# New costs for the SyncE transfers in a planned Trainium2 kernel, and another order of all its tasks

## The chip, the cores and the metric

The kernel runs on one core of a Trainium2 chip. The core has a matrix engine (TensorE, PE in the profile; its weight loads are PEld), VectorE (DVE), ScalarE (ACT), GpSimd (POOL) and SyncE (SP), which issues transfers. Each engine takes its own instructions in order; they wait for each other through semaphores. The metric is the time of one execution on the device in microseconds (us), as the median of three runs. A profiled execution gives a span, which is the time from the first to the last instruction of the program.

## The reference

Two layers are applied twice, A (attention with a recurrent memory) and B (a gated feed-forward), each to the layer-normed activations and with a residual. The weights are the same both times.

```python
def _A_ref(x, mem0, Wq, Wk, Wv, Wo, seg_len):     # x: 1 x 2048 x 512
    mem = mem0                                    # 8 rows
    for s in range(n_seg):                        # 64 segments of 32 rows
        h = concat([mem, x[segment s]])           # 40 rows
        q, k, v = h @ Wq, h @ Wk, h @ Wv          # 32 heads of 128
        p = softmax(mask(q @ k.T * scale))        # memory rows are seen by all, the rest is causal
        o = (p @ v) @ Wo
        mem = o[:8]; outs.append(o[8:])           # the next segment needs this memory
def _B_ref(x, w_gate, w_up, w_down):              # 512 -> 1792 -> 512
    return (sigmoid(x @ w_gate) * (x @ w_up)) @ w_down
x = x + _A_ref(_layernorm(x), ...); x = x + _B_ref(_layernorm(x), ...)
x = x + _A_ref(_layernorm(x), ...); x = x + _B_ref(_layernorm(x), ...)
```

A segment of A can't begin before the segment ahead of it has given its eight memory rows. This makes a chain of 64 segments in each of the two passes.

## The kernel before

**Steps.** The two passes run interleaved: in step t (`emit_step`, 70 steps) the first pass works on segment t and the second on segment t-6 (`LAG`). From step 6 to step 63 both are present and a step has 80 columns, 40 of each. Before and after that it has 40. After every fourth step of a pass comes the feed-forward of the 128 rows that are then complete (`ffn`), whose gate, up and down weights are streamed from HBM in pieces by GpSimd (L1140, L1141, L1165).

**One step.** The 32 heads go in six groups. For each group TensorE makes Q and K (L923), ScalarE copies them to the tile `qku` (L944, carried out at L1285), TensorE makes the scores (L958), VectorE and ScalarE the softmax (L972 to L989), TensorE transposes it (L1001), two copies spread it into `ptsb` (L1279 or L1287 on VectorE, L1277 or L1285 on ScalarE), TensorE multiplies it with V (L1028), ScalarE copies the result into `otsb`, and TensorE multiplies it with the output weights (L1046). The last copy of a step (L1059, VectorE) writes the new memory rows into the input `hT` of the next step.

**V.** The V rows that do not depend on the memory are made ahead, for whole blocks of 128 rows (`v_pass`, `v_half`, `v_strip`), and stored in a scratch tensor in HBM, `scr` (L727, L764, L774; those of L727 and L764 are issued at L1281). In its step each such set of rows is loaded from `scr` into the tile `vsb` (L892, "rows" below, 24 rows of 1024 elements). The V rows that depend on the memory are made in the step by the matmuls of `strips` (L837), copied to `sst` and moved to their partitions of `vsb` by transfers (L903, "strips"). L1028 needs both. There are three `vsb` tiles, and a step uses two, so that a row transfer waits until L1028 of an earlier step has read its buffer.

**Saved columns.** In steps 0 to 5 the Q and K of 14 columns of the second pass are made along and saved (`kx`, written to the tensor `xq` at L952). In steps 6 to 11 they are loaded again (L871) and copied into `qku`. The blocks of x are loaded at L814.

**Order.** Nothing is emitted in the order in which `trace` names it. Each call `pl.add(engine, duration, function, r=, w=, lat=, nb=, slow=)` makes a task, with the tiles that it reads and writes, its issue time, for a transfer its latency until the data has landed (`lat`), its bytes (`nb`), and a share `slow` of the time for which weights are still streaming that is added to the latency. `Planner.plan` decodes the string `SEQUENCE` into a priority for each task. `forward` then plays all tasks through: whenever an engine is free, it takes the ready task with the highest priority, and a task is ready when what it needs has ended by the planned durations and latencies. So the emitted order on each engine follows from both, the priorities and the costs. The choice between ScalarE and VectorE for a copy, and between SyncE and GpSimd for some stores at the start, falls in the same way. SyncE is planned with at most eight transfers on their way.

**Fillers.** Where the plan leaves TensorE idle for over 250 ns at the start or after a thin stretch, `warm` puts matmuls of a constant tile in (L1271). They do nothing but keep the array busy.

The lines of the costs before:

```python
{"SP": 450, "POOL": 590} if boot else (400 if n == XS else 650)    # L727, store of V rows to scr
lat=1750.0 if b < 2 else None                                      # L814, x block; None is 4000
lat=3000.0                                                         # L873, kx
pl.add("SP", 375, ...), lat=2425.0, nb=nx * 2048, slow=1.0         # L892, rows
pl.add("SP", 600, ...), lat=2800.0, nb=nr * 2048, slow=0.6         # L903, strips
```

Of the kernel before, what the change touches and what calls it, by code (L numbers as in the profile page):

```python
# [20 lines left out]
P = 128  # L21
MEM = 8
SEG = 32
L = MEM + SEG
LW = 2 * L
XS = 24
# [28 lines left out]
;AsOfI9&h>01L}@xdvLQE|92eUGM9vk>p6h1lsKkB^29CMlL#^u9wB%1;X1aT-yCr)h^vqn{ccqtPEvUe^t*qOXz+z_UfSyR<kN<%R+NE9&QHjj<pdSp3CgCAC3h8^)yHKKrAEbzD2^vK#Fyn>oiLZcveBE4i53u  # L55
SI7gpgiO8+0q_g7z1dxxZw32ChqmxZj3++bjM=LtK&{Rp{IoUSeU|-iQe-$^np+3y*U~5|vmroI2|{3Q%S6U<M8?h}*J#6~ePFa&ILsP!iu)7M5zN}^;Hu*SkiWLt*l(;S-RciTt7j;!OclX8)R5sKu~O_HD!r1+
jCIF}*+yMG1QFSz)a{%7Adp3>lEB~B=MtoL428l7*eg@LBRPg-nsQ6v)y9;i>$(UC(aBy(o!AIwl~I$cgq8W9Wp}GPr0+oN?n!J3?D*{wW@2=s#eTk~wKe8QE?=WSX#u&mTeg#vYy?Rp>C(hv&bz%?pbf?=b}MF_
eO$W+#>2rveRa&s{$Nm5nNlpBy-Iu*4?_dWf<v!4+(q#pEwMk%5Z|67@u_WH)YDU;(8!QhOARUI@Ev$x`u@x*jByPk@sLpOC&1#RVOJh$lj(bC1d{d*)swiuXTt}spz40;rOBLuJ`uD7xa-ZjG9Qx~Yhb)>0}@{&
oqYugl(zT%&|W5_&rYr^Hs5H<BVhK1#NR7T%m9eQo~P9*BixidoIm{z#)5bD<m=G2*^@zhpvf?l?}6Jkr-@v|hw1`SI+F<rNj>J`)+W5o*fp+rSu#D|P&7rp7aWAwxHxlgc;$!At7$s0u0dZ^>Q%|9b*OUG)Kd|V
a#F;OGGzIJe_kq^-IMRF%TQ8m0V;(+iN9N8`!Z(hCvYtwB_4$P8RayXB@L8NkY6qJJ9Vova$FJfB0xcz@`1-gjGZ4TwAWQm9lDkE4=en>PiYLyavFTU=8P;Ni7bkPUF~y{NT^sK?@nuP27qn2(Tbj=pUwpTd&wfr  # L60
;vn+p55I)krt8@^*b8H{Na;xc%~``DuWGkVk<Cm}R-CrQWZ`4;;dgT-{$Z*q<}1{&a1+T=@Slz8iZkI!S}eXyae}BoI*xmDI$28yNQRH9k!T9ZU8In??!x!83EW{8W>+1ejosWwfq3Lztd9o%7-t8kDJi>B>kDo4
eA-oCu|dTIF0BkK8reW}fQfx1j)VzS{gg`C!j&(&+O4wh3;F|@Yg{6^dgkYz%bglXMBOw2Aix2(ih;~{9G(66p~AZp=^Nq#Y<a-pr#!Nxtbx3PEZ7H%#WJDmq&nPd-PGt|Ywo<+&t{#{Nt7b0Bro&6of$r~>_v*_
9ras2J?7d?<RRtFusz7ln=>9h5h*N8NdQP6gP0BT$`55r91aYXaXIs2J1S9u?PTNkIa-q3w6YsU45c`#(ULHdpV*82^@euSg-ey#+=oxlHqN7Sf1StR14}+-7k8vg31_)kSvwhIt{pJ=_g5=kZQ~5BiM8FSEM?TX
pew0R6uF&$gf2qG;Cc)$gt=i7B24}e^N7Qq&$QN9wh~FBXT(58?j$v!`}J+dR4M!OsI0aUFo&@+%@9*A1JMR{zI-ZkUTG_yKFpSCWC|QpET?5wHOAjV30aJg%K)6k1;l(IHMtS0l^gj!<sKedb<zs8Ls?wEXh6fR
xIk(E4Pn<UMX;SrNj!<=L3?t84g=8fclD#7yj1VnuQ)7HbC`_QE)1?eLH#3Zs3Qz9P-FL^xU7?_nXg_&$@O|uYAp9j|9NE5<U^nSVLoL=j>3j*lkzI%LR*H|&8kw_$5gp?6JL~o9)n@O3E#B~6h{smtD*LmlPLl+
G)A(n^s3wmvf_OiM#;Ngxr1tczZY9^2K5F~+diMwKC<0q_9-D-?iBWAN2@Jb7?MIXZ~`4_A-p_6!#<yO+!|<JJR+7irZ5M&yA<Iz1FdFEKGcduJ{LT}-2}46EMz%$^iB^sUP)`!E}d~eNTAfS;*erAk5GI~-fu0Q
?tH?Yg9_>H51&URf=fln2iLSM#P<G!+*l~+VXq1GfL;wEH-t>+$CK>q|7AAW!K5&nTclK_^z_V|Pt5?6sx7=#!p?+HGHaVhxd7;2Y$g6b?NBextlu{vpKQccKk!JtuXVKECWP|BDTc853cOD3QGVnb9JqZ1tdu%V
(F#;aw#){W_e{TALuP$|+*!(5dgLq81pH~AIj~fxqm^SFug_03%!Io0zYcU6%6B-5wRf!*EbmtDIL~~cGF|bSH=VwIq}W1F#F1KM9jgBp2yZBeIu?Jow<5O@oeu!)<<XGbXy^Ob;9C8D-gJ&zYCuxwmb5y_Yuf|D
7}wYFM?_6qWGcocqWEiarEaf%+&a9>Nk@OiNST3--;KAuM-5qY{1Q+<8)iR5Jt6C-L9oao+>myjNFjM7j8j9PA~cs5f@q+c`~5|qVl(NbM|YPcXdG)V-5L?3%+132)cvOuQ;?s*9n*Y$5^E=pKHsnhWP94xv3$1l
{XWA(vcG(Wg$1AFZX6f5U#qQpeM|B<8bL${mhLb{$Ixi#f?S5+AV_YMnGfxG)<ff!h((g449-Smtw=wOZWkkg>uW)2WNMhfFJSHVC?tCk(?;@LzKGlgIE1?URop&83VKNohpzu{3JOTpCEFV`?4(@PY7Y-WB5YO0  # L70
ge1R4!Cyl^sxzc>&O1xr9_FkR4C~_hE)m<kIDeNr+P+l?<|(tG^eJSe@>nSVP1KStG3Wu7t&p0~?GSXWKO>@O65VygJ{3P<pZbSC=Sq)aT?c1M&8#?h{Zrs!9OPF~Te}`);5oSv-?cM~my)puyS*6Gz;xD>&JgL6
f99KHg26|z9O9LYxhpg4(Ba}7LeK=2jggLK);OgbD)Q3g(mCF!Ht)VJ8XTImVtKXw^`@-vnN>GjmB_NeEvZjb++L-$j}5u+ozFGq>I>^W!Auz5`B7)W9%cKS#G&tH;tEb=RaKBlF@N1j&mUYoKr)t@4+O36`eZtX
iDt+VkT-z}d%<+E5>F1vkR~DDGfJ)N`x(@+z9)3Wb*LtmnRKVF%TnAfE%cf0Rs!7}iA`{XIyYH_-38im5MI=KA2>-7@vH4RPL1gyE2mkiDQ|nGb2VI|8)hSq9+QTZ6`_Zc1EQ5a*}0hf7zFN<(+~HIYO_M`1yDLg
;jR2VHx=(yXnloyVX|?t3?OHu$&Dg(-DZKM)brogA-E$daDdz93la4qafiHI8xPrgB{kAz-z^Tu+Y=!8lOov50Py+FLNkih=5_oPD<*_{&-Ra!G3<ss69&hs!WK2ZtkowL`0=K=w|gHqfBoC0Q28sf`szN$y}`gx
kc2YE1b^><;3lZh#sw@SU>9%;g84-{)@CWwy4L1n%Z?@!*e%WaA60tbAwO&g?ub}MWxk3aNIU4_xv=)i*Rt894VY!mHgb?=u%xLt!_z^fTyDX9%e2>G^a$E`Tj1~C^lx&X+MA9fSK#GmAVdK51M$*Ia6~{jsS7NP
qIM`znQ>9Pxk=T7yRDB$1`zD06*ZYT()R%<H6p1C9O1?Hxo+7jaR{W4SU*?NFLMZ1>$-dCt}<Y{!NNv5R;vQneRZw*OS#~6$cP2SLVl@F?9#Ot&Uu6eyqlqgYPz{;R+|ySzeT8bOx~7x*n4ptRNJ{2!S`|@%A<WV
&K^P&(BSiUsT&T(wamON<vNZXjp=g6zy%}u2SBja4|y6sv23s_)@G=(sQY!g6ItpKa@+V+Iy$+7ZCUQtU5u6oD3ovRcI~g}gb`__5EIOs(A|uDXe&nw-Z0Sg4*{0~XQY2?Z)s_wS?uLSCSiQyNf|D2<M8>M_Phy~
l&(%&GK;0>m-W!f;$z8l>eM?cMyU`$r4M_7qE<p8*j7)FY=dIdd^`_xy|c`l9;UsRpPctVXoN~qK^G5j0wjC>V1CI4_lM$Y$+Gh5T)A~SQsFpYTJ1TKfwS`&c^oSrd|iv`Y^t%_2MY88dQFY6{=uDZ$It)nX&Q*b
5~$(|eq~y`Z}Eg(p)oZ%DJrL$?b~gPaKUM1n&odK{$O*|u$}UE>~-ybtz|KVon*3!S`t;F8=^$4rf0e*m!kb)Rt|3#X4e{gx7_S$;mpaiB_F9;rX=NH$AfP{E#(F+0|MC*_w8!=2f4pQ6uq{GqR8cRpKieqE>lc9
yg(7S3B>|v5rq};V4)w>R*$xRb8tz?#SsW1gS0IfGsn9Jy#@t<ufLaus^Q;2JfZqYO4x7jjJ>I;0~wb(zMC6d^NeNgAa3&G<=|T4Ec!gc6|FvO*$@zJ+f!r=0_ULM6r$$e%$7nBjIHu-sZro(7$1~aqH`wS)-OuW  # L80
{+mk!BvS}f^3loSi5ZruZusL~;=l?m$B%7j&2N)X0bacAg@%`RmM^!|f9J7nm1i7b(&z@J^#22Jdl?22yNV^WQ4D@wWl)!k2bLUFMYhr=CF9wbc%1@hX<e0%<q02J)b%WBy)KMIbz%VHzqPVD*~WL+_-dPc3k#~M
WqjsYp{><~v`tgNn~#Z0`Q;jflJelAc3~vr1wbsFlAdiY@3>UDBY^(9Eg3cGhx51IJ~&7o^e0=*cl&a!_*^l&E|uQOk)bM~_G_Mnr4ag$Paf~f5+z$f3az65APw>TuvKV|C^F(MSnY`UD1}92R_j<4DN|a4-DhX!
zJEHNIg3bioKJV54ndGl|9=to>{~@dv06wfY4#EO9!G1Q04LKqY8<0c)`EBdsZ-bN$=UXc4115<p!k<{+fonl8uGELTtt+BBnv|`$U*Vzn-r=7goM_3c4OXk;bVJ1@!}4G4XKkpLsr+ygTK*??$3|i?KFdg1XQ0D
Z_~HfW(&zo4?e{S>CgE(@tpqYK%Y~5MjgVEf!U0Y0XwSS&dGoKdK<hnVUDGM>1yhkpfD2AQ&lT*?r+ahN*TV6q_6~HZ<^{q3;E>=st<F@zb!DQ1ck!;MF_aR?OoIz9R?+%JJ{(S`CR|9Lh0HJoy8XHL9b=J^sngt
BAM@2iepOh4q6Ny_5hNTBEBrCDHto}0TOFSVeCNPCRs+UYrsQfp5VsAbY1!&_iVoB664azU}iZ{{%cTTyK(Y|fh1i`LOigZRtXYOiq_}GHDAnmV0|4vp2UDU4ym*2d`oKtNRKmUnt|Tzcc%32UNrR_qWEr*s}y<@
_w5%QvSS$$Pk9G=gwHK$EZ^8IrDS3)T*bz$amn&zIEYUcftc4d6(gP89~GN-&J8F@Pfk^VFHOx>S~%_f;>!I<c88F}^m3Z_pFRk#33GY>$1zjyXQQOlIeyz>CMBM-?5&UBAK;+%jZD-FCFu;!y|)A|jLeHE5%?|z
D+KX&`1g2$BX19j0BM;#yL_OVErdZTl3_}GmPuw`goJy5D=2k+zY||~^NkAEEf;&*!~2_+(V>M&M3QRJ1MiMD;bY&4^;7?|81U-xuZ<#B^6Ak6x-B3_1uhvg$@dp}SArA7AwaiC1*Xp~N*fiAiNhyhq~2S5?5BWR
Hn)s(s^P`!%;StBs0Z=dg3|4TN$Sno_d28Rl)%_3)Lv}oJXK)JPH!l7UqXOWraL;}T1bBSN|N<Tm=yH{GGwyK2SB6IG!P23f5oKJ81RJhJ{&B_>QeFTy2mpqi!T{ZZ70M!!jTIZtx8;Hy>zndA%4$uzRBj|5mh-4
GVG#Mnf-F8;t$fa;h*2>HOsW3m1#dzyc5!8C^j!VkC`D(0eHwFW%P$goCXjNi_-8Y0%)wy@VJ|jatlVBtarW{zNy`L&_~sQ{**^F2i~+wVZ5>L_GCZSJi59y7W;c}3()6{DjG5?HI0T0u}j3$lQWXjkywU5LuV=W
;pIjJe)F+93SjcWX{PO1*8iP(y{pkU>wSy}vz=|Y70|uh;!pS%Ft86nIYI1Z9urWikohb4fpC_w^P>i;@i;DsOCYP^;7<q(KEn-8S%8$}vH(ND4ZV$o(mdW90<r7)L_lOh?CT<ly;-B&9#?ic-I+8$F?(Hyahvgt  # L90
<fsyZpo^y~;MhAKv(-Mo1LStkt0^fT$w7QiMBMmEXpxAq$GNj<KZ#;rKwzNGJ^1AayX!tq-0)Dx*}VTALVxT1trNk8adW5O9SERf25ro`u`h(X4ULpde<B3_4d2Z&0%Ku1OBO;kIT77sq>8$C-wG8ao6XYS%48R}
_|gTLU>_PS>8L~Mil=Q50*O^Di#S>GL9p|}!LtZbc%WJ3b#;)yJIx}w@B@+$^PdMky1+6#ll|l|fv=R8(L|T2U!fJw1iXP@kv|ZC?8Tp;#4P&<ej=7_l#xmW=cz_Nk;A36MlutxZ%n3#8hBidXUboGhbrV0d!LqP
9xzAQ(-Zd&y}_5`hG^`Gw>ryv|17uDhspjsr|D*4V<d$}nK;;O`jFTA^-^KHH$kA1^tIOScC1{YQ)g@K8A&7MVXZ*ht#<5KrBc3>SmC}(M<OqE{q!i$3y*-*{s)fBwhWt({gE&KIQT9`n*yn&ns{CVq+WCIN962k
y&0PGK}(xZx2q4r!R+TLZS3XJa;6mEI<-7V$=`16g+qefBI1VAfa?q4uke&936N?96AvC(HCW#kD%V&4lvL%t(+mw?Z2bcDpFr)wy2PzYBrtO087>97Zkkx&@8rOq*~%Ouj?);**JT%QNmR@dY#yIb!<be5)>;2)
b9!_~e`QYSYszG<yb;W^!Ki|4>6;e0OrQ|w9cd=_=!BCSXRrMsYbG@15T+~!n+;rr0sg>NOadJGSnPJR+;~{I4>xS$cyug3A`I)QL)*&d<<;O3FN(atVB3X`wBzWR3`$l$qc+{9!4{8&c`koXmrTXeXDhzvy&JiJ
y#rp5#pe7u<Hg|ibJcUKMfEKdlZB3{(X*qk?wC5BShIbp-k8R5{_!z{+~FE)KT?57Er8DQKea|Fig_=qnmt$K4ZC!2<r8lrV3*(KFBT@PJ(6+3Jp^DVF^PyfoE#<eb&)=0=HR{&bw#U-Gl7GJ=?u`!md-jhLhOTs
A}u)t+OP)^&OmaUwTXH&5{cqXZL&`gdvGdI=ZF_-qr7?n;lxdZj9Fw7FVZIZDi9r8plwgl3>Bhm<Rta*y%y*+@PL=lqa&t91ps<#H28%kG5c9s!xRMuQ-b(esOr4NhcpTM0|3F4?HtST9Nd+&f(XRe2qiJcZV1e<
# [367 lines left out]
class Kern:  # L465
# [237 lines left out]
    def v_pass(self, tile, keys, pieces, boot=False):  # L703

        nc, pl, DC = self.nc, self.pl, self.DC
# [645 lines left out]
```

## Time and profile before

| | |
|---|---|
| median of three runs | 1791.44 us (1787.53 to 1792.42) |
| the profiled execution | 1786.9 us |
| its span | 1785.1 us |
| TensorE busy | 1762.3 us, 40081 matmuls |
| VectorE, ScalarE, GpSimd busy | 1171.3, 1170.9, 575.6 us |
| strips, `vsb<-sst` (L903) | 516 transfers: 464 of 32 KB, 48 of 64 KB, 4 of 48 KB |
| rows, `vsb<-scr` (L892) | 508 transfers: 460 of 48 KB, 48 of 16 KB |
| granted TensorE clock | 0.999 |

Matmuls overlap in the records: each is shown with its full latency of about 0.2 us, while the next one starts when the array can take it. Busy time is the union of the records. A wait is put down to the semaphore that came last. "issue" stands for idle time in which the engine waited for nothing that the profile shows. SPq is SyncE's queue: the time of an entry is that of the issue, not of the transfer.

### The profile page before, as it was taken

To read this page: it belongs to the slowest core of one execution; us is meant where nothing else is said; L and a number is where in the kernel's file an instruction comes from. 1 tells how busy PE (TensorE), PEld (TensorE's weight loads), DVE (VectorE), ACT (ScalarE), POOL (GpSimd) and SP (SyncE) were. 2 spreads that over 40 slices of the span, in tenths; PEclk is the share of its full clock that TensorE was granted. 3 is DMA by queue.
4 is the path that set the end of the run, shared out by engine and by line. 5 is a ranking of instruction groups with operands and counts; after the bars stand their busy time and mean duration, and the time that the engine had idled before them with its cause. 6 is when DMAs were issued, how large, how long until landed. Compare 5 with 4: busy or idle time off the path is not lost.

```text
span 1785.1 us, 92363 instructions
## 1 busy us (share of the span) xinstructions
PE 1762.3 (99%) x40081; PEld 1510.4 (85%) x40081; DVE 1171.3 (66%) x4002; ACT 1170.9 (66%) x3040; POOL 575.6 (32%) x831
## 2 busy tenths in 40 slices
PE   9999999999999999999999999999999999999998
PEld 4578788989888898889888898989888888889886
DVE  4376666677576666666666677657766766666675
ACT  6676766666666666766666666666666666666664
POOL 5313032422333242323324241333325132333432
PEclk9999999999999999999999999999999999999999
DMA  9835354644555464545546453555546454554543
GB/s 347 276 89 153 84 163 136 192 115 131 160 157 156 131 183 130 142 131 161 163 126 196 131 169 101 157 157 168 153 132 195 113 147 126 156 158 131 170 131 107
DMA packets 135305, 273.43 MB, mean 153 GB/s; under 512 B 30778, under 2 KB 68546, under 8 KB 134898
## 3 DMA queue, kind: packets, MB, share of 16 engines
q0 software_dynamic: 56384, 182.30, 34.8%
q1 hardware_dynamic: 78514, 85.22, 16.6%
q8 instruction: 314, 5.14, 1.2%
q14 instruction: 93, 0.76, 0.1%
HBM read 221.78 MB, written 27.07 MB: 139 GB/s over the span
## 4 chain that ended last, share of the span: by engine, by line
PE 91%; DMA 3%; DVE 2%; SPq 2%; ACT 1%; issue 1%; POOL 0%; ACTq 0%; POOLq 0%
PE bank L923 30%; PE bank L1046 17%; PE bank L1148 11%; PE bank L713 8%; PE bank L837 7%; PE bank L1171 5%; PE bank L1028 4%; PE bank L958 4%; PE bank L1001 2%; DMA vsb<-sst 2%; SPq L903 2%; PE bank L1271 1%; PE bank L673 1%; PE bank L1116 0%; DMA kx<-xq 0%
## 5 line engine op out<-in xcount | busy, mean ns | idle before, releaser
L923 PE MATMUL bank<-hT,wq_sb 128*128 128x80 bf16 (+3 forms) x8960 | 614.9, 198 | 1.0 <-DVE hT L1059 0.6
L923 PE MATMUL bank<-hT,wk_sb 128*128 128x80 bf16 (+3 forms) x8960 | 614.8, 198 | 0.8 <-issue 0.8
L1285 ACT CAST qku<-bank 128x480 bf16<-128x480 f32 (+4 forms) x770 | 387.5, 507 | 220.2 <-PE bank L923 183.0
L923 PEld LDWEIGHTS <-wq_sb 128*128 128x128 bf16 x8960 | 452.4, 99 | 26.5 <-issue 13.7
L923 PEld LDWEIGHTS <-wk_sb 128*128 128x128 bf16 x8960 | 446.9, 99 | 1.2 <-issue 1.2
L972 DVE TENSOR_TENSOR st<-bank,cst 40x240 f32<-40x240 f32 (+2 forms) x768 | 277.4, 367 | 169.7 <-PE bank L958 162.8
L1046 PE MATMUL bank<-otsb,wo_sb 128*128 128x80 bf16 (+1 forms) x8960 | 363.5, 198 | 3.3 <-ACT otsb L1285 1.8
L1046 PEld LDWEIGHTS <-wo_sb 128*128 128x128 bf16 x8960 | 336.8, 99 | 18.5 <-issue 3.8
L1140 POOL DMA_DIRECT2D wg<-in_B_w_gate_dram x217 | 163.9, 755 | 281.5 <-PE bank L1148 79.1
L1141 POOL DMA_DIRECT2D wu<-in_B_w_up_dram x217 | 164.2, 757 | 262.6 <-PE bank L1001 70.2
L1285 ACT CAST otsb<-bank 128x480 bf16<-128x480 f32 (+3 forms) x420 | 198.7, 483 | 72.2 <-PE bank L1028 48.2
L1165 POOL DMA_DIRECT2D wd<-in_B_w_down_dram x217 | 153.8, 709 | 199.2 <-PE bank L1171 48.5
L982 ACT ACTIVATE st<-st 80x240 f32<-80x240 f32 (+3 forms) x420 | 158.6, 381 | 30.6 <-DVE st L979 28.8
L984 DVE TENSOR_REDUCE small<-st 80x6 f32<-80x240 f32 (+3 forms) x420 | 151.2, 363 | 35.7 <-ACT st L982 33.9
L1148 PE MATMUL bank<-xnT,wg 128*128 128x128 bf16 (+2 forms) x1784 | 171.6, 218 | 0.3 <-DVE xnT L1287 0.3
L663 POOL TENSOR_TENSOR small<-small,cst 128x1 f32<-128x1 f32 (+1 forms) x80 | 45.1, 565 | 392.1 <-DVE small L662 389.2
L1148 PE MATMUL bank<-xnT,wu 128*128 128x128 bf16 (+2 forms) x1784 | 171.3, 218 | 0.2 <-issue 0.2
L958 PE MATMUL bank<-qku 128*128 128x80 bf16 (+1 forms) x2240 | 160.7, 198 | 0.8 <-ACT qku L1285 0.4
L979 DVE TENSOR_TENSOR st<-st,small 80x240 f32<-80x240 f32 (+3 forms) x420 | 153.9, 369 | 4.0
L989 DVE TENSOR_TENSOR pb<-st,small 80x240 bf16<-80x240 f32 (+3 forms) x420 | 153.1, 369 | 4.3
L977 DVE TENSOR_REDUCE small<-st 80x6 f32<-80x240 f32 (+3 forms) x420 | 151.1, 362 | 4.3
L1028 PE MATMUL bank<-ptsb,vsb 104*128 104x80 bf16 x2048 | 138.3, 199 | 6.5 <-DMA vsb<-sst 3.1
(105 smaller groups left out, 2409.9 us busy)
## 6 DMA issues: line engine op xcount, KB each, us to landing
wg<-in_B_w_gate_dram POOLq DMA_DIRECT2D x220, 256.0 KB, 4.3
wu<-in_B_w_up_dram POOLq DMA_DIRECT2D x220, 256.0 KB, 4.3
wd<-in_B_w_down_dram POOLq DMA_DIRECT2D x220, 256.0 KB, 4.2
vsb<-scr SPq DMA_DIRECT2D x460, 48.0 KB
vsb<-sst SPq DMA_DIRECT2D x464, 32.0 KB
scr<-vst SPq DMA_DIRECT2D x112, 96.0 KB
wv_sb<-in_A_Wv_dram SPq DMA_DIRECT2D x8, 512.0 KB
wo_sb<-in_A_Wo_dram SPq DMA_DIRECT2D x10, 384.0 KB
```

Source lines behind the costliest of these rows:

```text
L923: nc.tensor.matmul(o_ap, lhsT=W[:, c, h * P:(h + 1) * P], rhs=mv(c), start=(c == 0), stop=(c == DC - 1))
L958: nc.tensor.matmul(s_all(SB)[:, w0 + i, :], lhsT=fview(qku[:, i, 0, 0:1], [(1, P)]), rhs=qku[:, i, 1, 0:ncol], start=True, stop=True)
L972: pl.add("DVE", dve_ns(n, True), lambda gsz=gsz, hs=hs, st=st, SB=SB, pj_=pj_, npj_=npj_, mk=mk, idx=idx: nc.vector.tensor_tensor(out=st[p ...
L979: pl.add("DVE", dve_ns(n), lambda gsz=gsz, hs=hs, st=st, mx=mx: nc.vector.tensor_tensor(out=st[pr, hs], in0=st[pr, hs], in1=mx[pr, hs].uns ...
L982: pl.add("ACT", act_ns(n), lambda hs=hs, st=st: nc.scalar.activation(out=st[pr, hs], in_=st[pr, hs], func=ACTF.Exp, scale=self.scale), r=s ...
L1028: nc.tensor.matmul(fview(OB[:, o:o + 1], [(ncol, 2), (1, L)]), lhsT=self.vsb[halves[u // 8]][0:64 + L, j, (u % 8) * P:(u % 8 + 1) * P], rh ...
L1046: nc.tensor.matmul(WB[:, c * ncol:(c + 1) * ncol], lhsT=self.wo[:, h, c * P:(c + 1) * P], rhs=otsb[:, hl, 0:ncol], start=(h == 0 and c == ...
L1140: pl.add("POOL", 760, lambda wg=wg, fs=fs: nc.gpsimd.dma_start(out=wg[:], in_=self.wgv[:, :, fs]), r=[("wo", self.H - 1)], w=[gk] + bt, la ...
L1141: pl.add("POOL", 760, lambda wu=wu, fs=fs: nc.gpsimd.dma_start(out=wu[:], in_=self.wuv[:, :, fs]), r=[("wo", self.H - 1)], w=[uk] + bt, la ...
L1148: nc.tensor.matmul(gu[:, 2 * i + k, 0:n], lhsT=W[:, c, i * P:(i + 1) * P], rhs=xnT[:, c, rw], start=(c == 0), stop=(c == DC - 1))
L1165: pl.add("POOL", 760, lambda wd=wd, ip=ip: nc.gpsimd.dma_start(out=wd[:], in_=self.wdv[:, 2 * ip:2 * ip + 2, :]), w=[dk] + (["boot"] if se ...
L1285: nc.scalar.copy(out=dst, in_=src)
```

## The change

The issue times and latencies of the SyncE transfers are changed, and the string of priorities is replaced by another one of the same tasks. No tile, buffer, matmul or transfer is added or removed by the text; what the planner makes of it (the order on all engines, the engine of each copy, the fillers) is all that differs.

```diff
 SEQUENCE = r"""
-;AsOfI9&h>01L}@xdvLQE|92eUGM9vk>p6h1lsKkB^29CMlL#^u9wB%1;X1aT-yCr)h^vqn{ccqtPEvUe^t*qOXz+z_UfSyR<kN<%R+NE9&QHjj<pdSp3CgCAC3h8^)yHKKrAEbzD2^vK#Fyn>oiLZcveBE4i53u
...
++2Ak*GWXNbtuIcEuH|^H74br`XYi{)?D>nt2;izt8~(1Gv8^*?8;dI9`DXwC
 """
...
-                pl.add(("SP", "POOL") if boot else "SP", {"SP": 450, "POOL": 590} if boot else (400 if n == XS else 650),
+                pl.add(("SP", "POOL") if boot else "SP", {"SP": 450, "POOL": 590} if boot else (430 if n == XS else 710),
...
-        pl.add("SP", 430, lambda: nc.sync.dma_start(out=xb[:], in_=self.x_in[b * P:(b + 1) * P, :]), w=[("xs", i)], lat=1750.0 if b < 2 else None, boost=(self.boot() if b < 2 else 0), nb=P * self.D * 2)
+        pl.add("SP", 430, lambda: nc.sync.dma_start(out=xb[:], in_=self.x_in[b * P:(b + 1) * P, :]), w=[("xs", i)], lat=1750.0 if b < 2 else 5300.0, boost=(self.boot() if b < 2 else 0), nb=P * self.D * 2)
...
-                       r=[("xq", t - LAG, lo)], w=[("kx", p) for p in range(lo, hi)], lat=3000.0, nb=P * (hi - lo) * w * 2)
+                       r=[("xq", t - LAG, lo)], w=[("kx", p) for p in range(lo, hi)], lat=3500.0, nb=P * (hi - lo) * w * 2)
...
-                    pl.add("SP", 375, lambda j=j, s=s, row=64 * i + row + lo, h0=h0, vh=vh, r0=s * XS + lo, nx=nx: nc.sync.dma_start(
+                    pl.add("SP", 430, lambda j=j, s=s, row=64 * i + row + lo, h0=h0, vh=vh, r0=s * XS + lo, nx=nx: nc.sync.dma_start(
...
-                        r=[...], w=[("vx", j, vh, i)], lat=2425.0, nb=nx * 2048, slow=1.0)
+                        r=[...], w=[("vx", j, vh, i)], lat=2700.0, nb=nx * 2048, slow=0.9)
...
-                    pl.add("SP", 600, lambda i4=i4, i=i, vh=vh, j=j, lo=lo, k0=k0, nr=nr: nc.sync.dma_start(
+                    pl.add("SP", 632, lambda i4=i4, i=i, vh=vh, j=j, lo=lo, k0=k0, nr=nr: nc.sync.dma_start(
...
-                        r=[(sb, 0), (sb, 1)], w=[(name, j, vh, i)], lat=2800.0, use=[sb], nb=nr * 2048, slow=0.6)
+                        r=[(sb, 0), (sb, 1)], w=[(name, j, vh, i)], lat=3100.0, use=[sb], nb=nr * 2048, slow=0.6)
```

## The prediction

> **What bounds the kernel now.** I read the page's busy shares first, then TensorE's waits, then the transfer queue's waits, then two short stretches of the timeline.
>
> ```profile
> span 1785.1 us, 92363 instructions
> PE 1762.3 (99%) x40081; PEld 1510.4 (85%) x40081; DVE 1171.3 (66%) x4002; ACT 1170.9 (66%) x3040; POOL 575.6 (32%) x831
> ...
> PE   9999999999999999999999999999999999999998
> ...
> PEclk9999999999999999999999999999999999999999
> ```
>
> TensorE is busy in every slice at the full granted clock, so the end is set by its own work plus its idle time, 1785.1 - 1762.3 = 22.8 us. The changed kernel issues the same 39,974 useful matmuls (40,081 less 107 that only keep the array warm, L1271), so an order can win or lose only in idle time and in those fillers. Who ended the idle time (us in total, times, longest):
>
> ```profile
> PE bank L1028 <- DMA vsb<-sst: 3.1, 8, 0.8
> PE bank L1028 <- DMA vsb<-scr: 2.6, 3, 1.9
> PE bank L1116 <- ACT oxT L1285: 1.8, 5, 0.4
> PE bank L1046 <- ACT otsb L1285: 1.8, 3, 1.4
> PE bank L1046 <- issue: 1.3, 1, 1.3
> PE bank L673 <- issue: 1.1, 1, 1.1
> ```
>
> Late V rows in vsb head the list with 5.7 us. A matmul is shown 0.20 us long while the next starts 0.04 us after it, so each gap is about 0.16 us longer than shown: 11 x 0.16 = 1.8, together 7.5 us. The 1.4 us before L1046 is a transfer too: ScalarE stood just before it at a copy of saved columns,
>
> ```profile
> 292.64 0.42 ACT L1285 COPY qku<-kx 128x84 bf16<-128x84 bf16 x2 [1.66 <-DMA kx<-xq]
> ```
>
> so late kx costs about 1.55 us. How V rows come late is seen at the longest wait, on the SyncE queue and on TensorE:
>
> ```profile
> 900.45 1.26 SPq L1281 DMA_DIRECT2D scr<-vst  x2
> 901.80 0.40 SPq L892 DMA_DIRECT2D vsb<-scr  x1
> 902.25 1.07 SPq L1281 DMA_DIRECT2D scr<-vst  x2
> 903.37 0.46 SPq L892 DMA_DIRECT2D vsb<-scr  x1
> 903.87 1.10 SPq L903 DMA_DIRECT2D vsb<-sst  x1
> ...
> 905.91 0.34 PE L1028 MATMUL bank<-ptsb,vsb 104*128 104x80 bf16 x5 [1.91 <-DMA vsb<-scr]
> ```
>
> The queue issues back to back; the row transfer issued at 901.80 lands 4.1 us later, while the plan gave it 0.375 us to issue and 2.425 us to land (plus up to 2.3 us while weights stream).
>
> **The change, part by part.**
>
> *The costs alone.* They are numbers for the planner; no instruction takes longer on the chip for them. A transfer that is planned to land later is issued earlier relative to its reader. The shift is (430+2700)-(375+2425) = 330 ns for rows (with 0.9 instead of 1.0 of the weight term, so at worst 330-230 = 100 ns), (632+3100)-(600+2800) = 332 ns for strips, 500 ns for kx, 1300 ns for x blocks from L814.
>
> *What the shift covers.* From the trace I took each transfer's time from the start of its issue to the last update of its semaphore before that is used again, and subtracted what the plan allowed, by the old and by the new numbers, after the first 60 us. Of 516 strips, 65 were late against the old numbers by 17.3 us in sum, and 21 would be against the new, by 3.9. Of 506 rows, 38 by 19.5, and 31 by 10.9. Together 36.8 falls to 14.8, or 40%. For kx 2.6 falls to 0.7, 27%. If stalls scale with lateness, V stalls fall from 7.5 to 3.0 (-4.5) and kx stalls from 1.55 to 0.4 (-1.1). Bounds: -9.1 if all go; 0 if another transfer is late in the place of each, or beyond that a loss, as in the rival below.
>
> *x blocks (L814).* Old plan 4.43 us, new 5.73; measured median 4.17, longest 6.24. One wait at L1148 hangs on such a load (at 1049.78, 0.32 us shown): -0.5 at most, and I take it.
>
> *Why issue is slow, and a rule against the change.* A strip's issue takes 0.587 us in the median, yet 94 of the 1383 issues on SyncE took over 0.9 us, up to 1.99; at 93 of these 94 a packet of the instruction queue (q8, 314 packets in the page) starts within the issue or 1.5 us before, against 277 of the 1231 others. The Trainium skill (Runtime: NRT & Kernel Launch, section Instruction fetch mechanics) says that a sequencer streams its code in 16 KiB blocks and that crossing a boundary is mostly hidden. By that rule the longer latency covers nothing and the costs bring 0. By the row a fetch anywhere slows SyncE's issue by 0.3 to 1.4 us, and one such delay is more than the shift of 0.33. I follow the row: the shift helps, but a strip that meets a fetch and has no other margin still comes late. That is why 40% remain.
>
> *Fillers.* The build has 94 filler matmuls for 107. Counted in 128 columns, those outside the start fall from 214 to 168, so 46 x 128/2.4 ns = 2.45 us less on TensorE's in-order queue. The largest cut is in step 2, where the chain of waits has
>
> ```profile
> 113.72 1.89 PE bank L1271 x9
> ```
>
> and the new order has 4 (0.80 us). A filler gone saves its time if the data is there, and nothing if TensorE then waits as long: 0 to -2.45, I take half, -1.2. The clock stays: no idle time shown is over 1.9 us.
>
> *The new order.* On TensorE 2520 of 4202 tasks keep their relative order, and a task moves by 2 to 4 places on average (84 at most), so weights and halves keep their stage. It costs where no other work can be put under the longer lead: the chain has vsb or kx transfers at 127.85, 166.74, 217.56, 263.15 and 290.24, in steps 3 to 10, where the feed-forward work is thin. Four such places at 0.33 us give +1.3; 0 if the cover is found, and 18 thin steps (0 to 11, 64 to 69) x 0.33 = +6.0 if nowhere. I take +1.3, since only in these places a transfer is in the chain now. The other TensorE waits (oxT, otsb without kx, hff, xn, hT, the two "issue") come to about 10.5 us; a new order draws them anew, and I put 0 with +-3.
>
> *Moved between engines.* 42 copies go from ScalarE to VectorE (14 scaled ptsb copies among them; 0.47 us there against 0.32 here). Both are a third idle, and 42 x 0.32 = 13 us over 1785 lie in that; without cover the most is one copy in each of the steps concerned, already in the +-3. Two boot stores go from SyncE to GpSimd (some 0.6 us each), whose weight issues wait for TensorE anyway. SyncE has 1381 issues for 1383. It stands in order: it waits 348.8 us in 98 waits for L1028 to free vsb,
>
> ```profile
> SPq L892 <- PE bank L1028: 348.8, 98, 10.5
> SPq L903 <- ACT sst L1285: 207.9, 52, 9.9
> ```
>
> and behind a row transfer that waits so stand strips, scr stores and kx loads. An earlier row issue is useless unless the buffer is free, which is part of why I don't take the full -9.1.
>
> **Sum.** -4.5 -1.1 -0.5 -1.2 +1.3 = -6.0 us on the profiled execution: 1785.1 to 1779.1 span. That execution took 1786.9, so 1.8 us lie around the span, and 1780.9 is expected for its like. The median of the three runs is 1791.44, 4.5 above the profiled one; I carry the difference over: **1791.44 - 6.0 = 1785.4 us**.
>
> **The rivals.**
>
> *The late ones just change places (no change).* For it: the longest stall is 1.5 us beyond the allowance, made of several slow issues in a row, and 0.33 us doesn't cover that; the fetches fall elsewhere in a new order, and the present order's 7.5 us is one draw of them. Against it: 44 of 65 late strips were late by less than the shift. It gives -4.5 and -1.1 reduced to a third, and the fillers lost to waits: -1.9 -0.5 +1.3 = -1.1, so 1790.3. Also here: the order is a stored list, and if it does not place transfers earlier, the new costs do nothing.
>
> *Nearly all DMA stalls go (much faster).* -9.1, -0.5, all fillers -2.45, no price: -12.0, 1779.4. For it: steps in the middle have ample feed-forward work to put under a transfer. Against it: 0.33 us is less than a fetch.
>
> *SyncE's queue turns into the limit (slower).* A row transfer set earlier in the in-order queue meets a vsb buffer that L1028 still reads; strips behind it are late. Price: a step with both layers issues eight strips and eight rows; if in each of the 58 such steps one such block leaves 0.25 us uncovered, that is 14.5 us, less 6.0 won: +8.5, 1799.9. It decides from 0.10 us per step (5.8 us eats the gain); it is slower by 0.3% from 0.20. For it: the 98 waits above. Against it: mean idle on that queue is large, and strips have their own readiness.
>
> **How the numbers follow.** 0.3%, 5.4 us, is about what a measurement of this kernel can tell from no change. The forecast has 0.50, with its own range 1781 to 1790 (bounds +-3 from other waits, +-1.3 fillers and +-1.3 price, put together); half of it lies beyond 0.3%, 0.26 faster and 0.24 within. The no-change rival has 0.10, of which 0.05 within, 0.02 slower, 0.03 faster. The much faster one 0.24, all faster, since the present stalls were drawn with an order that allowed too little everywhere. The slower one has 0.16, all slower. That makes 0.53 faster, 0.29 within, 0.18 slower. The range 1778 to 1797 leaves out most of the slower rival and the far end of the faster one.
>
> **What would show it.** In the profile after: the two rows "L1028 <- DMA vsb" together at 3 us or below instead of 5.7; the kx wait before L1046 under 0.5; TensorE's idle total near 17 us for 22.8, busy time lower by the fillers; SyncE's issue medians unchanged (0.59 strips, 0.36 rows), which shows that only places moved. The prediction is wrong if TensorE's idle grows at waits on copies by ScalarE or VectorE, if new waits on vsb stand in steps that had none, or if stalls without any releaser ("issue") grow.

## The result, and the profile after

The changed kernel takes 1778.1 us (median, 1774.95 to 1781.16) against 1789.45 us for the kernel before, measured beside it (1784.34 to 1792.42). The ratio is 0.9939 [0.9921, 0.9958], about 11 us or 0.6%. The forecast was 1785.4, with a range from 1778 to 1797: the sign was right, the gain was nearly twice the predicted 6.0 us, and the time lies 0.1 us inside the lower end of the range.

The two profiled executions are 8.8 us apart (span 1785.1 to 1776.3). The profiled execution of the kernel before was 2.5 us faster than its median of 1789.45, that of the changed kernel was its median. So the profiles show 8.8 us of a gain of 11.

The page of the changed kernel, busy time and the clock that TensorE was granted:

```profile
span 1776.3 us, 92287 instructions
PE 1757.0 (99%) x40068; PEld 1509.3 (85%) x40068; DVE 1173.7 (66%) x4044; ACT 1162.7 (65%) x2998; POOL 576.2 (32%) x833
...
PEclk9999999999999999999999999999999999999999
```

TensorE's idle time fell from 22.8 to 19.3 us, its busy time from 1762.3 to 1757.0. Busy time fell though the useful matmuls are the same. Fillers count as busy, and they hold TensorE for 1.5 us less, taken from each start to the next. And a gap of under 0.16 us doesn't show as idle, because each matmul is drawn 0.20 us long while the next could start after 0.04.

The page's tenths hide one thing about the kernel before. Its mean clock of 0.999 stands for one stretch of 3.4 us at half the clock, close to the end (columns: stretch, its length, busy time with instructions of PE, PEld, DVE, ACT and POOL, granted clock, DMA share, GB/s):

```profile
1772.70:1776.10 3.40, 3.40 (x51) 2.15 (x48) 1.02 (x4) 0.97 (x4) 0.04 (x1) 0.50 0.51 157
```

The profile of the changed kernel has none. Such a stretch takes at most 1.7 us of TensorE's work, but it isn't where the 8.8 us come from: the table below has the same lead before it and after it. The medians don't hang on it either. Of the runs of the second set below, those with a clock of 1.000 alone have medians of 1788.8 us (kernel before, six) and 1776.6 us (changed kernel, three), 12.2 apart.

What ended TensorE's idle time in the changed kernel (us in total, times, longest). L1028 of before is L1054 here, L1046 is L1072, L892 and L903 are L918 and L929:

```profile
PE bank L1142 <- ACT oxT L1311: 2.1, 6, 0.4
PE bank L699 <- DVE xn L690: 1.8, 2, 1.2
PE bank L949 <- issue: 1.5, 3, 1.0
PE bank L1197 <- DVE hff L1180: 1.1, 1, 1.1
PE bank L1054 <- DMA vsb<-sst: 1.0, 4, 0.4
PE bank L1072 <- ACT otsb L1311: 1.0, 3, 0.4
...
PE bank L984 <- ACT qku L1311: 0.7, 2, 0.4
...
PE bank L1027 <- DVE pb L1015: 0.5, 1, 0.5
```

The waits for V rows have gone from the head of the list to its middle: 1.0 us for strips, and 0.2 more in one row transfer below the list's limit, where it was 3.1 and 2.6. All four listed ones lie before 400 us. Before, nine of the eleven lay after 490 us.

What SyncE's queue waited for in the changed kernel, and how long its issues take (ns, minimum/median/maximum):

```profile
SPq L918 <- PE bank L1054: 349.0, 92, 9.3
SPq L929 <- ACT sst L1311: 200.1, 50, 10.9
```

```profile
L929 SPq DMA_DIRECT2D vsb<-sst x516: 507/587/1982, 64.4 to 1745.0; - x172
L918 SPq DMA_DIRECT2D vsb<-scr x508: 263/355/1909, 46.1 to 1736.2; - x170
```

The queue waits as long for its buffers as before (348.8 us in 98 waits then). The issues have the same medians and the same longest ones; after the first 60 us, 95 of 1325 take over 0.9 us, against 94 of 1325 (the prediction sets its 94 against all 1383). No transfer became faster: the median from issue to landing is 2.78 us for strips (2.70 before) and 3.32 for rows (3.34). Only their places moved. The planner did not see a gain in that: played through with the costs of each kernel, the new plan ends 1.0 us later than the old one (1761.4 against 1760.4 us).

**Where the time was won.** I took the end of each step, which is the start of the copy that writes the new memory rows (L1059, or L1064 where only one pass is present), in both traces. A negative number is time won up to there:

| time in the kernel before, us | after minus before, us |
|---|---|
| 103.3 | -0.5 |
| 277.0 | +0.3 |
| 302.8 | -2.1 |
| 426.0 | -1.3 |
| 584.1 | -2.8 |
| 888.6 | -3.1 |
| 917.6 | -6.0 |
| 1196.2 | -5.9 |
| 1505.2 | -6.8 |
| 1674.7 | -6.9 |
| 1749.2 | -8.9 |
| end of the span | -8.8 |

The first 277 us won nothing. Three places give most of the rest. Between 277 and 303 us lies the 1.4 us wait behind which kx stood. Between 889 and 918 lies the wait of 1.9 us for V. In the thin last steps, from 1675 to 1749, the kernel before waited 0.8 us for `xn` and 0.8 without any releaser, and not for V.

**How much time stands ahead of a reader.** For each V transfer I took the time from the start of its issue to the start of the L1028 (L1054) matmuls that read it, in three profiles:

| transfers with a lead of | before | changed | changed, second profile |
|---|---|---|---|
| strips (516), under 3.5 us | 29 | 19 | 22 |
| strips, under 4 us | 52 | 39 | 43 |
| rows (508), under 5 us | 10 | 5 | 8 |
| strips between 280 and 1510 us, median lead | 7.63 us | 7.46 us | 7.62 us |

The lead as a whole is what it was. Only the tight places have become fewer, by a quarter to a third among the strips under 3.5 us, by a fifth to a half among the rows. The table flatters the kernel before a little, since a reader that is held up by its transfer counts as one with more lead.

### The profile page after: what moved, and what is told of

Its sections match the earlier page's. It is cut to its first block, busy times and chain, and to the rows that moved or that the text cites. A ratio compares the mean times of both kernels' runs of the same rounds, so it can differ in the third digit from the quotient of the medians.

```text
span 1776.3 us, 92287 instructions
## 1 busy us (share of the span) xinstructions
PE 1757.0 (99%) x40068; PEld 1509.3 (85%) x40068; DVE 1173.7 (66%) x4044; ACT 1162.7 (65%) x2998; POOL 576.2 (32%) x833
## 4 chain that ended last, share of the span: by engine, by line
PE 93%; DMA 2%; DVE 2%; issue 1%; POOL 1%; ACT 1%; SPq 0%; POOLq 0%; ACTq 0%; DVEq 0%
PE bank L949 32%; PE bank L1072 16%; PE bank L1174 11%; PE bank L739 8%; PE bank L863 7%; PE bank L1197 5%; PE bank L984 4%; PE bank L1054 4%; PE bank L1027 2%; PE bank L699 1%; PE bank L1297 1%; DMA vsb<-sst 1%; PE bank L1142 1%; DMA wd<-in_B_w_down_dram 0%; POOL wu L1167 0%
## 5 line engine op out<-in xcount | busy, mean ns | idle before, releaser
L998 DVE TENSOR_TENSOR st<-bank,cst 40x240 f32<-40x240 f32 (+3 forms) x768 | 278.0, 367 | 167.3 <-PE bank L984 160.3
L1072 PE MATMUL bank<-otsb,wo_sb 128*128 128x80 bf16 (+1 forms) x8960 | 359.9, 198 | 1.2 <-ACT otsb L1311 1.0
L1072 PEld LDWEIGHTS <-wo_sb 128*128 128x128 bf16 x8960 | 335.1, 99 | 15.8 <-issue 2.6
L1054 PE MATMUL bank<-ptsb,vsb 104*128 104x80 bf16 x2048 | 136.5, 199 | 3.5 <-DMA vsb<-sst 1.0
```

The costliest lines, as they stand in the source:

```text
L998: pl.add("DVE", dve_ns(n, True), lambda gsz=gsz, hs=hs, st=st, SB=SB, pj_=pj_, npj_=npj_, mk=mk, idx=idx: nc.vector.tensor_tensor(out=st[p ...
L1054: nc.tensor.matmul(fview(OB[:, o:o + 1], [(ncol, 2), (1, L)]), lhsT=self.vsb[halves[u // 8]][0:64 + L, j, (u % 8) * P:(u % 8 + 1) * P], rh ...
L1072: nc.tensor.matmul(WB[:, c * ncol:(c + 1) * ncol], lhsT=self.wo[:, h, c * P:(c + 1) * P], rhs=otsb[:, hl, 0:ncol], start=(h == 0 and c == ...
```

## The experiments

Two sets of kernels ran, each beside its own runs of the kernel before (medians 1785.91 and 1789.87). The theory was that V transfers come late because a code fetch slows an issue on SyncE, and that the new costs and order put more time ahead of their readers. The rivals were that the late ones just change places, so that the gain comes from elsewhere, and that SyncE is slow for a reason of its own.

### What V transfers cost each order

The transfers that fill `vsb` (L892, L903) are left out of both kernels. The tiles are cleared once instead, so these two compute with zeros for V. The order of all else is unchanged.

```diff
+                    self.out_v.add(len(pl.tasks))        # ahead of L892 and of L903
                     pl.add("SP", 375, ...
...
+                if tk.idx in self.out_v:                  # in the loop that emits the tasks
+                    continue
                 got = tk.fn()
```

> The order of before with the row transfers (L892) and strip transfers (L903) left out, so that L1028 multiplies with V rows that never arrive and nothing can be late in vsb; the tiles are cleared once instead. Theory (late V rows are what the change won): the records of before put 8.0 us of TensorE's delays on vsb transfers, so 7 to 9 us less than before, ratio about 0.9955. Rival (the gain lies in other places of the order, and a late V row only hides another wait behind it): 3 us less or nothing, ratio 0.998 or more.

> The same left out of the changed kernel. Theory: only 2.2 us of late V rows are left in it, so it wins 2 to 3 us over the changed kernel (ratio to before about 0.9925), and the two kernels without V transfers are 3 to 4 us apart instead of 11. Rival (gain elsewhere): the two stay 8 us or more apart.

Measured: the kernel before without these transfers 1773.19 us, ratio 0.9926 [0.9909, 0.9943]; the changed kernel without them 1771.03 us, 0.9915 [0.9898, 0.9931]. The removal is worth 1785.91 - 1773.19 = 12.7 us in the old order. In the new one it is worth 1785.91 x 0.9939 - 1771.03 = 4.0 us. So 8.7 of the 10.9 us that the change wins in these units are gone when the V transfers are gone. Without them the two orders are 2.2 us apart and their intervals overlap. The 8.7 hangs on three ratios, each uncertain by 0.0017 to 0.0019, so it is good to about 5 us: enough to say that most of the gain is there, not enough to share out the rest. The removal does more than end the waits at L1028: the queue that carries SyncE's transfers moves 43 MB for 85, and the weight pieces land in 3.8 us for 4.3 to 4.4, in both orders alike.

TensorE's waits in the kernel before without V transfers:

```profile
PE bank L674 <- DVE xn L665: 2.0, 2, 1.4
PE bank L1119 <- ACT oxT L1290: 1.8, 5, 0.4
PE bank L1274 <- DVE small L574: 1.0, 1, 1.0
PE bank L1174 <- DVE hff L1157: 0.9, 1, 0.9
...
PE bank L674 <- issue: 0.3, 1, 0.3
PE bank L1004 <- issue: 0.3, 1, 0.3
...
PE bank L1049 <- ACT otsb L1290: 0.2, 1, 0.2
```

The removal took away more than the 7.5 us that I had put down to these waits, and more than the 7 to 9 us expected. What the rest is, is open. The wait for `otsb`, behind which kx stood, is 0.2 here and was 1.8, but it is 0.2 in another profile of the old order too, which has all its V transfers (the shifted one below). So the 1.4 us were a draw of the one profile. The waits without any releaser ("issue") come to 0.6 us here and came to 3.7. Whether they have to do with V transfers isn't shown: the changed kernel without them has 1.1, and the changed kernel without its later fillers, which has all transfers, has 0.7.

### Less time ahead of L1028 in the new order

In the new order the matmuls with V (L1054, the L1028 of before) of two of the groups of a step are placed up to 330 ns earlier, as far as the data they need by plan and the tasks that follow them allow. That was to take back what the costs gave. The fillers are computed ahead of the move.

```diff
+        for i in self.pvs:                                # tasks of L1054 with g in (0, 2)
+            tk = T[i]
+            first = max([T[d].start for d in tk.deps] + [T[d].start for d in tk.prev] or [0.0]) + 1.0
+            last = min([T[d].start for d in tk.succ] + [u.start for u in T if i in u.prev]) - 1.0
+            tk.start = min(max(tk.start + -330.0, first), last)
+        order.sort(key=lambda k: (k.start, k.idx))
```

> The changed kernel with the L1028 tasks of the first and the third group of each step (the first readers of each half of vsb) moved 330 ns of planned time earlier in TensorE's order, all else in the same order: the extra lead of the new latencies taken back. Theory: delays at L1028 by vsb transfers rise from 2.2 to 6 us or more and the time by 3 to 6 us (ratio to before 0.996 to 0.997). Rival (the lead in the order does not matter, the present stalls are a lucky draw): no change, 0.994.

Measured: 1777.49 us, 0.9954 [0.9938, 0.9969], and the wait for V in the profile is

```profile
PE bank L1054 <- DMA vsb<-sst: 2.0, 2, 1.1
```

Both expected figures were missed. The wait lies within what the changed kernel itself shows (1.0, 1.3 and 5.0 us in three profiles, below). By ratios the kernel is 0.0015 x 1786 = 2.7 us slower than the changed kernel, but the intervals overlap. It decides nothing, and the edit is the reason. The chip sees only the order. Of the 140 tasks that were moved in the plan, 81 keep their place in TensorE's order, because no other task of TensorE starts within these 330 ns, and 59 go up by one to three places. So little lead was taken back: 47 strips have a reader within 4 us, where the changed kernel has 39 and 43, and 19 within 3.5 us, where it has 19 and 22.

### The changed kernel without fillers after the start

```diff
-            if gap > 250.0 and on:
+            if gap > 250.0 and on and end < self.COLD:
```

> The changed kernel without the fillers past the start (28 places, 168 x 128 columns, 9.0 us of TensorE). Theory of the prediction (half of a filler's time is on the path): 3 to 5 us less than the changed kernel. Rival 1 (TensorE waits for the data anyway): no change. Rival 2 (the array's clock falls in the idle time): a granted clock below 0.99 and some us more.

Measured: 1777.6 us, 0.9946 [0.9927, 0.9966]; span 1776.6. The edit takes out 28 places as expected, but 189 x 128 columns instead of 168, because it leaves only the first filler of the start; at 2.4 columns a ns these are 10.1 us. TensorE spent 25.0 us from the start of a filler to the next matmul, and 10.3 without the later ones. The span stayed within 0.3 us of 1776.3. The clock and the waits of that run:

```profile
core 0: 1776.6 us, clock 0.997
```

```profile
PE bank L1142 <- ACT oxT L1311: 3.2, 9, 0.4
PE bank L699 <- DVE xn L690: 2.6, 3, 1.5
PE bank L1027 <- DVE pb L1015: 1.9, 5, 0.7
PE bank L984 <- ACT qku L1311: 1.9, 5, 0.6
```

Two things take the place of a filler. TensorE waits for the softmax, a copy or the layer norm instead: `oxT` from 2.1 to 3.2, `xn` from 1.8 to 2.6, `pb` from 0.5 to 1.9, `qku` from 0.7 to 1.9. And the clock falls. The mean of 0.997 looks like nothing, but it is three stretches of 3.4 us at half the clock (columns as above):

```profile
115.60:119.00 3.40, 3.31 (x84) 3.19 (x80) 1.95 (x11) 1.77 (x6) 0.75 (x1) 0.50 0.31 92
177.00:180.40 3.40, 3.40 (x32) 1.20 (x32) 0.53 (x2) 1.37 (x6) 1.19 (x2) 0.50 0.59 172
1764.20:1767.60 3.40, 3.40 (x92) 2.97 (x90) 0.96 (x5) 1.23 (x5) 0.64 (x1) 0.50 0.58 164
```

The changed kernel has no such stretch in its profile, and its clock was 1.000 in six of seven executions and 0.999 in one. Without the fillers it was 0.996 to 0.998 in all six. Three stretches can cost up to 3 x 1.7 = 5.1 us. The ends of the steps show both sides: at the end of step 5, at 176.7 us, this kernel is 0.8 us ahead of the changed one, and at the end of step 6, behind the second stretch, it is 0.7 us late. So that the time stays the same doesn't mean that a filler costs nothing. What the removal saves, new waits and the lower clock take back, and the run doesn't tell how much falls to each. Rival 2 was right about a lower clock and wrong about its size: 0.997, not under 0.99.

### The same two orders with the code shifted

If the late transfers of the old order are only a matter of where TensorE's code fetches happen to fall, shifting the code shifts the loss. Of the large filler at the start the first columns are issued as single 128-column matmuls instead of 512-column ones. That puts 128 more instructions on TensorE ahead of all steps in both kernels (64 matmuls and their weight loads), with the same columns to compute, and nothing else changes. It is half a block by an estimate from the run of issues below: there the fetches beside 80-column matmuls are 4.6 us apart, the time of some 123 matmuls with as many weight loads.

```diff
+                    big = n > 100
                     while n > 0:
-                        m = min(n, 4)
+                        m = min(n, 1 if big and n > 66 else 4)      # 56 in the changed kernel
```

> The kernel before with the first 85 of the 151 x 128 filler columns at the start issued as 85 single matmuls instead of in fours: the same array time while the first loads are under way, but 128 more TensorE instructions, so that every later code block of TensorE begins half a block elsewhere in the work. Theory (the order's allowance decides, code fetches only pick which transfer is late): within 4 us of before. Rival (the stalls of before are bad luck with where its fetches fall): 6 to 10 us faster than before, near the changed kernel.

> The same shift of 128 TensorE instructions in the changed kernel. Theory: within 3 us of the changed kernel, ratio to before 0.993 to 0.996. Rival (its gain is good luck with the fetches): back to 0.998 or more.

> The changed kernel unchanged, to stand beside the next three on one chip. Ratio 0.994 to before; vsb waits of TensorE at 2 us or less again if they are a property of the order, up to 5 us if each execution draws them anew.

Measured beside the changed kernel run once more:

| kernel | median, us | ratio | span, us | vsb waits, us (times, longest) |
|---|---|---|---|---|
| before, shifted | 1787.79 | 0.9986 [0.9972, 0.9999] | 1783.5 | 7.0 (10, 1.4) |
| changed, shifted | 1778.58 | 0.9943 [0.9927, 0.9958] | 1779.1 | 5.0 (7, 2.2) |
| changed, again | 1777.44 | 0.9939 [0.9922, 0.9957] | 1773.3 | 1.3 (3, 0.5) |

Old order, shifted:

```profile
PE bank L1028 <- DMA vsb<-sst: 4.9, 8, 1.2
PE bank L923 <- issue: 2.6, 4, 1.0
PE bank L1028 <- DMA vsb<-scr: 2.1, 2, 1.4
...
PE bank L1046 <- ACT otsb L1286: 0.2, 1, 0.2
```

New order, shifted:

```profile
PE bank L1054 <- DMA vsb<-sst: 5.0, 7, 2.2
PE bank L1142 <- ACT oxT L1311: 2.1, 6, 0.4
```

New order, run again:

```profile
PE bank L1054 <- DMA vsb<-sst: 1.3, 3, 0.5
```

Two things follow. One shift of the fetches doesn't take the gain away: with both shifted, it is 0.9986 - 0.9943 = 0.0043, 7.7 us, where unshifted it was 0.0061. And an order has weak places of its own. The V waits of the old order recur at four places in its two profiles, near 497, 673, 752 and 1521 us; only their sizes differ there (the 0.17 us at 672.82 is 1.24 when shifted). Three of the four readers have 2.9 to 3.9 us of lead in the plan, where the median of the strips is 7.9. The others of the 11 and 10 waits don't recur, and the longest, 1.91 us at 905.91, is one of those. The new order doesn't escape either: it waits near 391 to 394 us in four of its five profiles, and one profile of it shows 1.0 us of V waits, one 1.3, the shifted one 5.0, with 2.2 us in one place.

### What slows an issue on SyncE

This kernel computes nothing of the reference and writes zeros. It issues three sets of 48 transfers like a strip (16 partitions of 2 KB between two tiles on the chip): beside an idle TensorE, beside 1100 matmuls of 80 columns, and beside 190 of 512 columns.

```python
def moves(k, part):
    for i in range(48):
        nc.sync.dma_start(out=dst[32 * part:32 * part + 16, i, :], in_=src[k][0:16, :])
def stream(k, cols, count):
    for i in range(count):
        nc.tensor.matmul(acc[k][:, 0:cols], lhsT=w[:], rhs=x[:, 0:cols], ...)
moves(0, 0)
stream(0, 80, 1100); moves(1, 1)      # side by side
stream(1, 512, 190); moves(2, 2)      # side by side
```

> Nothing of the reference is computed, zeros are written. SyncE issues 48 transfers like a strip (16 partitions x 2 KB from tile to tile) three times: with TensorE idle, beside a stream of 80-column matmuls, and beside a stream of 512-column matmuls, which uses up its code about six times more slowly. Theory (a code fetch of TensorE slows SyncE's issue): nearly no issue over 0.9 us with TensorE idle, about 1 in 8 to 10 beside the 80-column stream (a new code block every 4.6 us), about a sixth of that beside the 512-column one. Rival (SyncE's own code or its eight transfers on their way make the slow ones): the same share of slow issues in all three.

Its issues in the three stretches (5 to 37, 38 to 76 and 79 to 113 us of the span), in ns:

```profile
L34 SPq DMA_DIRECT2D dst<-src x48: 573/587/589, 6.0 to 35.7; - x48
...
L34 SPq DMA_DIRECT2D dst<-src x48: 507/587/1670, 38.5 to 74.5; - x48
...
L34 SPq DMA_DIRECT2D dst<-src x48: 507/587/1512, 80.3 to 111.3; - x48
```

With TensorE idle, all 48 lie between 573 and 589 ns. Beside the many short matmuls seven take over 0.9 us, from 1001 to 1670; beside the long ones, which use fewer instructions in the same time, two (1088 and 1512). The page counts ten packets of the instruction queue:

```profile
q8 instruction: 10, 0.16, 0.6%
```

None of them falls into the first set, seven into the second and two into the third. The tenth lies between the second and the third set. Each of the nine has exactly one slow issue within 0.4 us, and no slow issue stands without one. SyncE itself runs the same code in all three sets, so the rival that it is slow by itself falls. A code fetch while TensorE works through its instructions adds 0.4 to 1.1 us to the one issue on SyncE that it meets. That the fetch is TensorE's is argued: the packets come only in the sets where it runs, and more of them where it takes more instructions. TensorE itself hardly feels them. Its matmuls in the two streams show next to no idle time before them (the last number, in us):

```profile
L38 PE MATMUL acc<-x,w 128*128 128x80 bf16 (+1 forms) x1286 | 82.2, 231 | 0.2
```

**How much of the lateness that explains.** For each listed wait for V, in the two profiles of the old order and three of the new one, I looked at the transfer that landed last and the four issues ahead of it on SyncE. In 21 of the 35 waits, with 12.7 of their 20.1 us, one of these five took over 0.9 us. With 94 slow issues in 1325, five in a row would hold one in some 31% of cases, which is 11 of 35. So slow issues are behind part of the waits. In the kernel before they stand at 5 of 11, with 1.6 of the 5.7 us. The longest wait, 1.91 us, isn't one of these: the "x2" entry of 1.26 us on the queue that the prediction shows two places ahead of it is two issues, of 0.52 and 0.70 us. There the transfer itself took 4.0 us from issue to landing, where rows take 3.34 in the median. Landing times that scatter are the other source, and the new latencies leave room for both.

### Not tried

New costs with the old order, and the old costs with the new order, were not run. The string and the costs work as a pair: with the new costs the old string gives a plan of 1787.3 us, and with the old costs the new string gives none. So it isn't shown how much of the gain the larger latencies bring and how much comes from having another order at all. Old-order readers placed later, the mirror image of the second experiment, were not run either.

## Why the prediction was right in sign and low in size

**V stalls, -4.5: the right mechanism, mis-sized.** This is the term that was too small. The share that stays, 40%, was about right: leaving the V transfers out is worth 12.7 us in the old order and 4.0 in the new one, so 31% is left. The list of waits points the same way over several profiles: 5.7 and 7.0 us in the two of the old order, 1.2, 1.3 and 5.0 in the three of the new one. It is the base of 7.5 us that was too small: with the V transfers gone the old order is 12.7 us faster. What makes up the rest isn't shown. V and kx together were put at -5.6, and the pair of kernels without V says -8.7, good to about 5. In the two profiles, by the starts of the matmuls, which also see gaps under 0.16 us, V lateness fell from about 8.0 to about 2.5 us. The shifted pair shows how much of that is the draw of one execution. The longest stall was also misread as the work of slow issues, as said above.

**A rule against a row: the row held.** The row (93 of 94 slow issues beside a packet of the instruction queue) was followed instead of what the Trainium skill says (Runtime: NRT & Kernel Launch, section Instruction fetch mechanics), that crossing a code block is mostly hidden. The run of issues alone bears the row out: 0, 7 and 2 slow ones for 0, 7 and 2 fetches. For TensorE the rule holds in that run (0.2 us of idle time in 82.2 us of matmuls); the cost falls on another engine. What the prediction did not see is that a longer latency also covers transfers that land late without a slow issue, as at 6 of the 11 waits before.

**kx, -1.1: the size fits one pair of profiles, by luck.** The wait for `otsb`, behind which kx stood, fell by about 1.2 us counted by starts. ScalarE's waits for kx, before,

```profile
ACT qku L1285 <- DMA kx<-xq: 2.4, 3, 1.7
```

have no row in the changed kernel. But in the second run of it ScalarE waits 1.0 us for kx again, and 1.1 in the shifted one, while the shifted old order has only 0.3.

**Fillers, -1.2: not decided.** I took half of the 2.45 us. The run without later fillers took out more than that and won nothing, but it lost clock as well, so it doesn't give the worth of a filler. The prediction's "the clock stays" held for the changed kernel, at 1.000. Its reason, that no idle time is over 1.9 us, isn't one: in the run without fillers none is over 1.5 us, and the clock fell three times.

**Price of the lead, +1.3: open.** In the first 277 us, where it was to be paid, the profiles of the changed kernel stand at +0.3, -0.4 and, shifted, -1.7 us. No experiment takes this term apart from the fillers and the waits for V there.

**x blocks, -0.5: nothing to be seen.** The wait on such a load at L1148 is not among the waits after. Two weight loads show in the new list instead, 0.4 us for gate weights and 0.2 for down weights, about what was won.

**The other waits, 0 +-3.** They drew new numbers, as said. In the lists `oxT` went from 1.8 to 2.1 us, `xn` from 1.3 to 1.8, `ptsb` from 0.4 to 0.7, and the stalls without releaser from 3.7 to 3.0. By the table, about 2 us were won in the last thin steps without any V wait there; nothing in the prediction named them.

**What would show it.** The two rows of `vsb` at 3 us or below: 1.2 (5.0 in the shifted profile). The kx wait under 0.5: no row. Issue medians unchanged: they are. Of the signs of being wrong, two came in part: waits on copies grew by some tenths, and the V waits at 96.5, 196.5 and 392.7 us stand where the profile before had none. Idle near 17: a miss, at 19.3, as busy time fell by 5.3 where only fillers were to fall. Gaps that busy time swallows are a part of that, and the stretch at half the clock before, which counts as busy, can be another.

**The rivals.** That the late ones just change places holds for single transfers and fails for the sum: the shifted pair is still 7.7 us apart. The rival in which nearly all DMA stalls go (1779.4) came nearest in time, but not by its own mechanism: the stalls don't all go (the new order still gains 4.0 us without V transfers), and they were dearer than its 9.1 to begin with. SyncE's queue did not become the limit: 349.0 us of waits for L1054 to free a buffer against 348.8, and no reader of V is held up for over 0.4 us in the profile after.

**The carry to the median.** The 4.5 us between the profiled execution and the median of three were of the right kind but too much: over seven runs the median of before is 1789.45, 2.5 above the profiled one.

## What to carry to other kernels

A planned order is as good as its costs at the worst place, not in the median: set a transfer's latency from its slow issues and late landings, and look for stalls that recur at the same place in several profiles. Leave the suspected transfers out of both kernels to see what they cost in all; the list of waits shows less, as small gaps hide in the busy time. Before calling a change of order a change in what the chip does, count the tasks whose place in the order really changed. Read the clock as stretches and not as a mean: 0.997 over this kernel is three stretches of 3.4 us at half the clock.

## What the runs showed that I had not expected

- A code fetch while TensorE runs slows one issue on another engine's queue: 0.587 us becomes 1.0 to 1.67 (nine fetches, nine slow issues), and in that run never without one.
- The runs without V transfers scatter less. The standard deviation of the kernel before is 3.4 us in the first set (14 runs) and 1.5 without V transfers (6); of the changed kernel 2.3 (7) and 0.6 (6). Part of the scatter goes with the clock: of the 14, the six at 1.000 have a median of 1783.2 us and the eight at 0.998 or 0.999 one of 1789.2. Which of the two brings the other isn't shown.
- With all fillers after the start taken out, no idle time shown is over 1.5 us, and yet the clock fell to half three times. The fillers kept it up.
